# Attention and GLU on one core: GpSimd raises 2 to a power for one score bank in most passes

## The chip, the core and the metric

The kernel runs on one core of a Trainium2 chip. The core has five engines, each with its own in-order stream of instructions: PE (TensorE, matmuls), ACT (ScalarE), DVE (VectorE), POOL (GpSimd) and SP (SyncE, which here only issues DMAs). They meet through semaphores. SBUF is the working memory; PSUM has eight banks of 128 x 512 fp32, into which PE writes. The metric is the device time of one execution in microseconds. Three runs of the kernel before gave a median of 909.52 us (908.95 to 911.22).

## What is computed

The reference, cut to what matters (S = 2048 rows, D = 640, 32 heads of Dh = 20, F = 1728):

```python
xn = layernorm(x)
q, k, v = split(xn @ wqkv)                  # 32 heads of 20
p = softmax(q @ k.T * 20 ** -0.5)           # per head, 2048 x 2048
s = (p @ v) @ wo
h = sigmoid(xn @ w_gate) * (xn @ w_up)
g = silu(h @ w_down)
out = x + s * g
```

The 32 x 2048 x 2048 exponentials of the softmax are the bulk of the elementwise work.

## The kernel before

**Setup.** x is loaded and normalised (statistics on DVE, L226 to L241, the apply on POOL, L245), transposed on PE, and the first projections are made.

**Passes.** The four column chunks of 512 queries (QC) times eight groups of four heads (NG, GH) make 32 passes. A pass has 16 key tiles x 4 heads = 64 score banks (PER_PASS), each one 128 x 512 matmul of K (21 rows) against q (L1035); there are 2,048 banks in all. The scores are scaled so that a probability is 2^(score/128 - 127). Each bank of scores in PSUM is turned into bf16 probabilities in SBUF, and PE multiplies these with V into the accumulator bank `oacc` (L1161), which a pass fills and `normalise` empties (L770).

**Who makes the exponentials.** ACT works in rounds: alternately three and two banks lie in one PSUM tile (`sc`), and one activation with Exp takes them at once (`act_exp`, L1058). Where DVE has room, `issue` scores one bank more in the round, into one of two PSUM banks (`misc0`, `misc1`, named spare or work) that all side jobs share too, and DVE makes 2^x in four operations (`dve_exp`): a maximum that reads PSUM into `dy` (L1069), a square and a cube on the low 16 bits of `dy` into `du` (L1074, L1078), and the sum that writes the bits of the bf16 (L1082). The last three read two operands in SBUF each. `dve_bank` picks the bank.

**Side jobs.** Between rounds PE does fill jobs: the projections of q, k and v, the gate and up matmuls (L643, L656), the down projection (L679), the output projection (L717). Each takes a misc bank, which DVE or ACT frees. The normalised gate result goes to DRAM (`gq_dram`, L699) and is read back (`gqr`, L712, four buffers) for the output, which POOL stores with an accumulating DMA (L726, L757).

**Normalisation of a pass.** `normalise` copies `oacc` to `oev` (L770), sends the denominators to DRAM (`den_dram`, L771), loads them in another shape (`den`, L776), takes reciprocals (L780), sends them to DRAM (`rec_dram`, L781), loads them four times as a broadcast (`rl`, L787), and multiplies (`oT`, L799). All these DMAs are issued by POOL. `oT` has NG + 3 buffers.

**The order.** A planner in the kernel's Python writes out each engine's order by hand. It keeps a clock for PE, ACT and DVE (`Engine`), with a cost for each operation (606 ns for a DVE operation on a bank, MM5 = 216 ns for a matmul of 512 columns, n x 512/1.2 + 52 ns for an activation of n banks, 3,400 ns from a DMA to its use), and emits an instruction when its inputs are there by these clocks. SP loads weights (`wg`, `wu`, L619, L621) and q (`qT`, L608) in the planned order. Where PE has room and has streamed less than ENOUGH (2,300) ns of matmul in the last 3,400 ns, `zero_add` (L1141) adds a matmul with a zero matrix to `oacc` (L1146); it does so only while a pass's accumulation is under way.

Of the kernel before, what the change touches and what calls it, by code (L numbers as in the profile page):

```python
# [15 lines left out]
P = 128  # L16
HEAD = 32
GH = 4
# [15 lines left out]
OCTAVE = 128.0  # L34
ONE = (127.0 + 80.0) * OCTAVE
LEAST = 128.0
EXP_BIAS = -127.0 / LOG2E
# [7 lines left out]
def kernel(  # L45
# [53 lines left out]
    pick = const.tile([P, GH], FP32, name="pick")  # L99
    zero = const.tile([P, P], BF16, name="zero")  # L100

    xnT = persist.tile([P, KD, S], BF16, name="xnT")
# [59 lines left out]
    with tc.tile_pool(name="setup", bufs=1) as sp, \  # L162
# [34 lines left out]
        nc.gpsimd.memset(eps_t, 1e-5)  # L197
        nc.gpsimd.memset(zero, 0.0)
        nc.scalar.activation(out=warm[:, 0:1], in_=eps_t, func=ACT.Sqrt)
        nc.gpsimd.memset(v_all[:, :, 0:VF, 0:1], 1.0)  # L200
# [168 lines left out]
    INTO = {"score": 100.0, "pv": 100.0, "fill": 100.0}  # L369
    WINDOW, ENOUGH = 3400.0, 2300.0  # L370
    PE_OUT, SEM = 260.0, 70.0
# [36 lines left out]

    act, dve = Engine(), Engine()
    pe = [0.0]  # L410
# [6 lines left out]
    def advance(until):  # L417
        while True:
            moved = act.run(until)
            moved = dve.run(until) or moved  # L420
            for x in sorted((x for x in timed if x[0] <= until), key=lambda x: x[0]):
# [244 lines left out]
    def down_job(tt):  # L666
# [25 lines left out]
        def finish():  # L692
            last = c == NQC - 1
            gq = kT_all[:, t4, :].bitcast(FP32)[:, 0:D] if last else d2
            nc.vector.scalar_tensor_tensor(out=gq, in0=made["t"], scalar=1.0, in1=d2, op0=ALU.add, op1=ALU.mult)
            if last:
                gq_last[t4] = gq
            else:
                nc.gpsimd.dma_start(out=gq_dram[tt, :, :], in_=d2)  # L699

# [6 lines left out]
    def out_job(tt):  # L707
        qc, t4 = divmod(tt, QC // P)
        yield "known", lambda: all((qc, g) in ot_cells for g in range(NG)) and (not tt or tt - 1 in out_cells)
        yield "wait", [ot_cells[qc, g] for g in range(NG)] + ([out_cells[tt - 1]] if tt else [])  # L710
        gqr = glu[0].tile([P, D], FP32, tag="gqr", bufs=4, name="gqr")
        nc.sync.dma_start(out=gqr, in_=gq_dram[tt, :, :])  # L712
# [50 lines left out]
    def normalise(qc, g, done):  # L763
        n = qc * NG + g
        cell = ot_cells[qc, g] = Cell()
        t = {}

        def s0():
            t["oev"] = wk.tile([P, QC], FP32, tag="oev", bufs=OBUFS, name="oev")
            nc.vector.tensor_copy(out=t["oev"], in_=oacc)  # L770
            nc.gpsimd.dma_start(out=den_dram[n, :, :], in_=t["oev"][0:P:32, :])  # L771
            at(dve.t + DMA_WAIT, s1)

        def s1():
            t["den"] = wk.tile([P, GH * QC // P], FP32, tag="den", bufs=2, name="den")
            nc.gpsimd.dma_start(out=t["den"], in_=den_dram[n, :, :].rearrange("j (r c) -> (j r) c", c=GH * QC // P))  # L776
            dve.add(250.0, [Cell(pe[0] + DMA_WAIT)], s2, 0)

        def s2():
            nc.vector.reciprocal(out=t["den"], in_=t["den"])  # L780
            nc.gpsimd.dma_start(out=rec_dram[n, :, :].rearrange("j (r c) -> (j r) c", c=GH * QC // P), in_=t["den"])  # L781
            at(dve.t + DMA_WAIT, s3)

        def s3():
            t["rl"] = wk.tile([P, QC], FP32, tag="rl", bufs=OBUFS, name="rl")
            for j in range(GH):
                nc.gpsimd.dma_start(out=t["rl"][32 * j:32 * j + 32, :],  # L787
                                    in_=rec_dram[n, j:j + 1, :].to_broadcast([32, QC]))
            at(pe[0] + DMA_WAIT + LANDED, s4)

        def s4():
            if g >= 3 and qc and not all(out_cells.get(tt, Cell()).t for tt in range((qc - 1) * 4, qc * 4)):
                at(pe[0] + 300.0, s4)
                return
            dve.add(606.0, [], s5, 2)

        def s5():
            oTs[qc, g] = wk.tile([P, QC], BF16, tag="oT", bufs=NG + 3, name="oT")
            nc.vector.tensor_tensor(out=oTs[qc, g], in0=t["oev"], in1=t["rl"], op=ALU.mult)  # L799
            cell.t = dve.t + 114.0  # L800
# [174 lines left out]
    KEEP_SPARE, KEEP_LATE, SPARE_END, next_round = 800.0, 400.0, 20 * PER_PASS, [0.0]  # L975
    BUFS, D_BACKLOG = {3: 4, 2: 4, 1: 3}, 2500.0
    NEEDED, NEEDED_LAST = 6, 12
# [61 lines left out]
    class Probs:  # L1039

        def __init__(self, banks, tag):
            self.n, self.left, self.tag = len(banks), len(banks), tag
            self.made, self.used = None, Cell()
            self.before = buffers[self.n].pop(0)
            buffers[self.n].append(self.used)
            for i, b in enumerate(banks):
                insort(ready_p[b % GH], (b, self, i), key=lambda x: x[0])

        def tile(self):
            self.ap = pp.tile([P, self.n, 512], BF16, tag=self.tag, bufs=BUFS[self.n], name=self.tag)  # L1050
            return self.ap
# [11 lines left out]
    def dve_exp(ps, b, begun):  # L1063
# [26 lines left out]
        return first  # L1090

    def issue():
        ci = chunk[0]
# [5 lines left out]
        if (ci > 1 and dve.backlog + max(0.0, dve.t - pe[0]) < D_BACKLOG  # L1099
                and all(c.t is not None for c in d_made[-2:-1])):  # L1100
            extra = dve_bank(taken)
            if extra is not None:
# [6 lines left out]
        if split:  # L1109
            score(split[1], extra)  # L1110
            issued(extra)
            give_bank(split[0], dve_exp(split[1], extra, begun))
            n += 1
# [5 lines left out]
    def pv_batch():  # L1119
# [68 lines left out]
    while pv_pass[0] < len(steps):  # L1188
# [46 lines left out]
        if zero_add(room):  # L1235
            idle = False
            continue
        soon = [q[k][1].made.t for q in ready_p for k in range(min(2, len(q)))]
        times = [until, pe[0] + 150.0] + [t + SEM for t in soon if t is not None]
# [32 lines left out]
    nc.vector.tensor_copy(out=rb, in_=rq.unsqueeze(3).to_broadcast([P, QC // P, GH, 32]))  # L1272
    oT = wk.tile([P, QC], BF16, tag="oT", bufs=NG + 3, name="oT")
    oTs[qc, g] = oT
# [9 lines left out]
    for bank, (t4, h) in zip(banks, units):  # L1284
# [5 lines left out]
        if h == 1:  # L1290
            if t4 % 2 == 0:
                pair = glu[0].tile([P, D], FP32, tag="gqr", bufs=4, name="ot").bitcast(BF16)
            ot = pair[:, t4 % 2 * D:(t4 % 2 + 1) * D]
# [30 lines left out]
```

## Time and profile before

One profiled execution took 909.74 us, of which 907.8 us are the span from the first instruction to the last. Its mean granted TensorE clock was 0.986.

| engine | busy us | share of the span | instructions |
|---|---|---|---|
| ACT | 871.8 | 96% | 837 |
| DVE | 839.6 | 92% | 1,480 |
| PE | 795.1 | 88% | 6,020 |
| POOL | 161.7 | 18% | 305 |

| group | count | mean ns |
|---|---|---|
| ACT Exp on three banks (L1058) | 358 | 1,575 |
| ACT Exp on two banks (L1058) | 359 | 1,148 |
| DVE maximum, square, cube, sum of a bank (L1069 to L1082) | 256 each | 681 to 683 |
| PE zero matmul (L1146) | 92 records of 129 | 388 |
| POOL apply in the setup (L245), 128 x 640 | 16 | 873 |
| POOL issue of `rl` (L787) | 124 | 522 |

A group's line gives its line in the kernel, engine, operation, out<-in with shapes and count; then the busy time and the mean of one; then the time that the engine sat idle just before the group, and what ended most of it. Activations overlap at their ends, so the two means exceed the busy time per activation. In the slices and windows a digit or number is the engine's busy time in that stretch; PEclk is the clock granted to PE, 1.00 being full. The chain is followed back from the last instruction to what released each step.

### The profile page before, as it was taken

The page shows a single profiled execution, that of the slowest core. Times are in us where ns is not written, and L with a number is a line of the kernel's source. Part 1 is how long each engine was busy: PE and PEld are TensorE (multiplying, and loading weights), DVE is VectorE, ACT ScalarE, POOL GpSimd, SP SyncE. Part 2 cuts the span into 40 slices and gives each one's busy share as a digit, 9 for nine tenths or more (in the row PEclk, how much of TensorE's full clock was granted, in tenths as well). Part 3 has the DMA queues.
Part 4 walks back from the last instruction along what each step waited for, and adds up shares of the span by engine and source line. Part 5 has one row for each costly group of instructions (what it writes and reads, how often), then busy time and mean ns, then how long its engine had stood idle before and what let it go on. Part 6 is the DMA issues. An engine that isn't in the chain of part 4 may idle for free.

```text
span 907.8 us, 16427 instructions
## 1 busy us (share of the span) xinstructions
PE 795.1 (88%) x6020; PEld 278.3 (31%) x6091; DVE 839.6 (92%) x1480; ACT 871.8 (96%) x837; POOL 161.7 (18%) x305
## 2 busy tenths in 40 slices
PE   5898989999888998989899988888989888989884
PEld 3334333222222332222233332222332232233232
DVE  7799999978999999998999998987999998999994
ACT  6999999988999999999999999999999999999992
POOL 7401111101111122111102221101112221111130
PEclk9999999977999999999999999999999999999998
DMA  8112231254232134313212243213112334200021
GB/s 312 46 41 80 74 98 35 69 166 136 70 78 56 36 106 62 72 43 90 52 35 77 77 72 78 63 34 73 34 52 76 90 62 88 57 19 14 14 59 41
DMA packets 105894, 64.36 MB, mean 71 GB/s; under 512 B 79982, under 2 KB 100002, under 8 KB 105594
## 3 DMA queue, kind: packets, MB, share of 16 engines
q1 hardware_dynamic: 95606, 47.21, 19.3%
q0 software_dynamic: 10208, 16.11, 7.7%
q8 instruction: 47, 0.77, 0.3%
q14 instruction: 33, 0.27, 0.1%
HBM read 50.45 MB, written 16.13 MB: 73 GB/s over the span
## 4 chain that ended last, share of the span: by engine, by line
ACT 55%; issue 17%; PE 14%; DVE 10%; POOL 1%; DMA 1%; SPq 0%; ACTq 0%; DVEq 0%; POOLq 0%
ACT p L1058 51%; PE sc L1035 5%; PE oacc L1161 3%; ACT tnh L650 3%; DVE dy L1069 2%; PE work L643 2%; DVE du L1074 2%; PE work L679 1%; DVE du L1078 1%; PE work L656 1%; DVE p L1082 1%; ACT td L690 1%; PE work L123 1%; DVE stats L226 1%; DMA den<-den_dram 1%
## 5 line engine op out<-in xcount | busy, mean ns | idle before, releaser
L1058 ACT ACTIVATE p<-sc 128x1536 bf16<-128x1536 f32 x717 | 828.9, 1361 | 10.3 <-PE sc L1035 4.5
L1035 PE MATMUL sc<-qT,kT_all 21*128 21x512 bf16 x1792 | 281.9, 386 | 74.8 <-ACT p L1058 68.8
L1069 DVE TENSOR_SCALAR dy<-spare 128x512 f32<-128x512 f32 x256 | 174.8, 683 | 26.0 <-PE spare L1035 24.1
L1035 PEld LDWEIGHTS <-kT_all 21*128 21x128 bf16 x2048 | 87.5, 91 | 308.5 <-issue 297.1
L1078 DVE SCALAR_TENSOR_TENSOR du<-du,dy 128x512 f32<-128x512 f32 x256 | 173.9, 682 | 1.8
L1082 DVE SCALAR_TENSOR_TENSOR p<-du,dy 128x512 uint16<-128x512 f32 x256 | 173.8, 681 | 1.8
L1074 DVE SCALAR_TENSOR_TENSOR du<-dy 128x512 f32<-128x512 uint16 x256 | 173.6, 682 | 0.7
L1161 PE MATMUL oacc<-p,v_all 128*21 128x512 bf16 x2048 | 159.1, 386 | 0.8 <-issue 0.5
L1035 PE MATMUL spare<-qT,kT_all 21*128 21x512 bf16 x256 | 99.1, 387 | 0.3 <-DVE gqr L723 0.3
L771 POOL DMA_DIRECT2D den_dram<-oev x31 | 18.0, 580 | 392.2 <-DVE oev L770 392.2
L679 PE MATMUL work<-wd,hT 128*128 128x320 bf16 x448 | 84.9, 302 | 1.2 <-DVE dy L1069 0.8
L643 PE MATMUL work<-xnT,wg 128*128 128x512 bf16 (+1 forms) x260 | 78.2, 387 | 1.5 <-DVE hT L660 0.4
L656 PE MATMUL work<-xnT,wu 128*128 128x512 bf16 (+1 forms) x267 | 76.5, 384 | 2.3 <-DVE dy L1069 0.9
L787 POOL DMA_DIRECT2D rl<-rec_dram x124 | 62.2, 522 | 54.7 <-DMA rec_dram<-den 45.7
L679 PEld LDWEIGHTS <-hT 128*128 128x128 bf16 x448 | 35.4, 97 | 48.1 <-issue 38.4
L1161 PEld LDWEIGHTS <-v_all 128*21 128x21 bf16 x2048 | 29.7, 90 | 64.3 <-issue 62.6
L660 DVE SCALAR_TENSOR_TENSOR hT<-tnh,work 128x512 bf16<-128x512 bf16 (+1 forms) x56 | 38.0, 679 | 6.0 <-PE work L656 3.5
L650 ACT ACTIVATE tnh<-work 128x512 bf16<-128x512 f32 (+1 forms) x56 | 40.9, 731 | 0.0
L781 POOL DMA_DIRECT2D rec_dram<-den x31 | 16.9, 546 | 133.0 <-DVE den L780 128.4
L717 PE MATMUL work<-wo_pad,oT 128*128 128x320 bf16 x192 | 35.5, 301 | 1.3 <-DVE dy L1069 0.7
L123 PE MATMUL work<-xnT,wqd 128*120 128x512 bf16 (+1 forms) x115 | 35.8, 406 | 0.8 <-DVE kd L499 0.4
L656 PEld LDWEIGHTS <-wu 128*128 128x128 bf16 (+1 forms) x280 | 23.1, 98 | 39.9 <-issue 25.9
(109 smaller groups left out, 538.8 us busy)
## 6 DMA issues: line engine op xcount, KB each, us to landing
wg<-in_B_w_gate_dram SPq DMA_DIRECT2D x52, 160.0 KB
wu<-in_B_w_up_dram SPq DMA_DIRECT2D x52, 160.0 KB
rl<-rec_dram POOLq DMA_DIRECT2D x124, 64.0 KB, 2.3
qT<-q_dram SPq DMA_DIRECT2D x31, 128.0 KB
gq_dram<-d POOLq DMA_DIRECT2D x12, 320.0 KB, 2.5
gqr<-gq_dram SPq DMA_DIRECT2D x12, 320.0 KB
kT_all<-k_dram SPq DMA_DIRECT2D x28, 128.0 KB
wd<-in_B_w_down_dram SPq DMA_DIRECT2D x1, 2080.0 KB
```

The source lines that it names most:

```text
L643: nc.tensor.matmul(psg[0:fsz, :], lhsT=wg[:, kd, 0:fsz], rhs=xnT[:, kd, cols], start=(kd == 0), stop=(kd == KD - 1))
L650: nc.scalar.activation(out=made["t"][0:fsz, :], in_=psg[0:fsz, :], func=ACT.Tanh, scale=0.5)
L656: nc.tensor.matmul(psu[0:fsz, :], lhsT=wu[:, kd, 0:fsz], rhs=xnT[:, kd, cols], start=(kd == 0), stop=(kd == KD - 1))
L679: nc.tensor.matmul(psd[:, 0:HALF], lhsT=hT[0:fsz, kf, t4 * P:(t4 + 1) * P], rhs=glu[1][0:fsz, kf, e0_:e1_], start=(kf == 0), stop=(kf == N ...
L787: nc.gpsimd.dma_start(out=t["rl"][32 * j:32 * j + 32, :], in_=rec_dram[n, j:j + 1, :].to_broadcast([32, QC]))
L1035: nc.tensor.matmul(ps, lhsT=kT_all[32 * j:32 * j + 1 + Dh, g, kt * P:(kt + 1) * P], rhs=qTs[qc, g][32 * j:32 * j + 1 + Dh, :], start=True, ...
L1058: nc.scalar.activation(out=buf.tile(), in_=ps, func=ACT.Exp, bias=EXP_BIAS, scale=exp_scale)
L1069: nc.vector.tensor_scalar(out=t["y"], in0=ps, scalar1=LEAST, scalar2=None, op0=ALU.max)
L1074: nc.vector.scalar_tensor_tensor(out=t["u"], in0=t["f"], scalar=CUBE_2, in1=t["f"], op0=ALU.add, op1=ALU.mult)
L1078: nc.vector.scalar_tensor_tensor(out=t["u"], in0=t["u"], scalar=CUBE_1, in1=t["f"], op0=ALU.add, op1=ALU.mult)
L1082: nc.vector.scalar_tensor_tensor(out=buf.tile()[:, 0, :].bitcast(U16), in0=t["u"], scalar=CUBE_SCALE, in1=t["y"], op0=ALU.mult, op1=ALU.add)
L1161: nc.tensor.matmul(oacc[32 * j:32 * j + 1 + Dh, :], lhsT=v_all[:, b % PER_PASS // GH, GH * g + j, 0:1 + Dh], rhs=buf.ap[:, i, :], start=(n ...
```

## The change

POOL takes one score bank in a pass, where the planner lets it. `issue` asks `pool_bank` first: it offers a bank only after the 40th round, with POOL free, and only if 400 ns for each bank left in the pass cover POW (20,000 ns, the planner's cost of the power) plus 3,000. Then DVE makes one operation (`px` = score/128 - 127, fp32, in SBUF) and POOL one: `pw` = 2 to the power `px`, with a column of twos as the base. `pw` has one buffer and is a kind of its own (0); `pv_batch` passes over such a bank until its planned end.

The DMAs of `normalise` (L771, L776, L781, L787) and the store of `gq_dram` (L699) are issued by SP instead of POOL. The accumulating stores stay on POOL. `gqr` has three buffers instead of four, and `oT` NG + 2 instead of NG + 3; `normalise` holds back its last step from the third group on (g >= 2, it was 3) until the chunk before is put out.

ENOUGH is 2,500 instead of 2,300. `zero_add` also runs when no accumulation is under way: into `oacc` if it is free, else into a free misc bank.

```diff
+POW = 20000.0
+    two = const.tile([P, 1], FP32, name="two")
+        nc.gpsimd.memset(two, 2.0)
-    WINDOW, ENOUGH = 3400.0, 2300.0
+    WINDOW, ENOUGH = 3400.0, 2500.0
-    act, dve = Engine(), Engine()
+    act, dve, pool = Engine(), Engine(), Engine()
-                nc.gpsimd.dma_start(out=gq_dram[tt, :, :], in_=d2)
+                nc.sync.dma_start(out=gq_dram[tt, :, :], in_=d2)
-        gqr = glu[0].tile([P, D], FP32, tag="gqr", bufs=4, name="gqr")
+        gqr = glu[0].tile([P, D], FP32, tag="gqr", bufs=3, name="gqr")
-            nc.gpsimd.dma_start(out=den_dram[n, :, :], in_=t["oev"][0:P:32, :])
+            nc.sync.dma_start(out=den_dram[n, :, :], in_=t["oev"][0:P:32, :])
...
-            if g >= 3 and qc and not all(out_cells.get(tt, Cell()).t for tt in range((qc - 1) * 4, qc * 4)):
+            if g >= 2 and qc and not all(out_cells.get(tt, Cell()).t for tt in range((qc - 1) * 4, qc * 4)):
-            oTs[qc, g] = wk.tile([P, QC], BF16, tag="oT", bufs=NG + 3, name="oT")
+            oTs[qc, g] = wk.tile([P, QC], BF16, tag="oT", bufs=NG + 2, name="oT")
-    BUFS, D_BACKLOG = {3: 4, 2: 4, 1: 3}, 2500.0
+    BUFS, D_BACKLOG = {3: 4, 2: 4, 1: 3, 0: 1}, 2500.0
...
+    def pool_exp(ps, b, begun):
+        buf = Probs([b], "pw")
+        t = {}
+
+        def copy():
+            t["x"] = pp.tile([P, 512], FP32, tag="px", bufs=1, name="px")
+            nc.vector.tensor_scalar(out=t["x"], in0=ps, scalar1=1.0 / OCTAVE, scalar2=-127.0, op0=ALU.mult, op1=ALU.add)
+
+        def power():
+            nc.gpsimd.tensor_tensor(out=buf.tile()[:, 0, :], in0=two.to_broadcast([P, 512]), in1=t["x"], op=ALU.pow)
+
+        first = dve.add(606.0, [Cell(begun + MM5 + PE_OUT - 100.0), *pow_made[-1:]], copy, 0, 114.0)
+        buf.made = pool.add(POW, [first, buf.before], power, 0, 200.0)
+        pow_made.append(buf.made)
+        return first
+
+    pow_made = []
+
+    def pool_bank(banks):
+        if pool.queue or pool.t > pe[0] + 1000.0 or any(c.t is None or c.t > pe[0] + 1000.0 for c in pow_made[-1:]):
+            return None
+        b = min((x for x in coming(GH) if x not in banks), default=None)
+        if b is None or b >= NB - PER_PASS:
+            return None
+        if 400.0 * (PER_PASS - b % PER_PASS) < POW + 3000.0:
+            return None
+        return b
...
-            extra = dve_bank(taken)
+            extra = pool_bank(taken) if ci > 40 else None
+            maker = dve_exp if extra is None else pool_exp
+            if extra is None:
+                extra = dve_bank(taken)
...
-            give_bank(split[0], dve_exp(split[1], extra, begun))
+            give_bank(split[0], maker(split[1], extra, begun))
...
+                if buf.kind == 0 and not (buf.made.t is not None and buf.made.t + SEM <= pe[0]):
+                    continue
...
-        if streamed() >= ENOUGH or not 0 < sum(pv_count[0]) < GH * KT:
+        if streamed() >= ENOUGH or (0.0 if mode[0] == "fill" else INTO["fill"]) + MM5 > room:
             return False
-        if (0.0 if mode[0] == "fill" else INTO["fill"]) + MM5 > room:
-            return False
-        nc.tensor.matmul(oacc, lhsT=zero, rhs=xnT[:, 0, 0:QC], start=False, stop=False, skip_group_check=True)
+        begun = 0 < sum(pv_count[0])
+        if begun and sum(pv_count[0]) < GH * KT or not begun and oacc_free[0].t is not None and oacc_free[0].t <= pe[0]:
+            nc.tensor.matmul(oacc, lhsT=zero, rhs=xnT[:, 0, 0:QC], start=not begun, stop=not begun, skip_group_check=True)
+        else:
+            free = [i for i in range(2) if banks[i].t is not None and banks[i].t <= pe[0]]
+            if not free:
+                return False
+            ps = psum.tile([P, QC], FP32, tag=f"misc{free[0]}", bufs=1, name="unused")
+            nc.tensor.matmul(ps, lhsT=zero, rhs=xnT[:, 0, 0:QC], start=True, stop=True)
         pe_do("fill", MM5)
         return True
```

In the changed kernel's line numbers the four DVE operations are L1074, L1079, L1083 and L1087, the copy to `px` is L1103, and the power L1106.

More of the change, by code (lines that the diff above doesn't have):

```diff
@@ L420, in advance @@
             moved = dve.run(until) or moved
+            moved = pool.run(until) or moved
             for x in sorted((x for x in timed if x[0] <= until), key=lambda x: x[0]):
@@ L775, in s1 @@
             t["den"] = wk.tile([P, GH * QC // P], FP32, tag="den", bufs=2, name="den")
-            nc.gpsimd.dma_start(out=t["den"], in_=den_dram[n, :, :].rearrange("j (r c) -> (j r) c", c=GH * QC // P))
+            nc.sync.dma_start(out=t["den"], in_=den_dram[n, :, :].rearrange("j (r c) -> (j r) c", c=GH * QC // P))
             dve.add(250.0, [Cell(pe[0] + DMA_WAIT)], s2, 0)
@@ L780, in s2 @@
             nc.vector.reciprocal(out=t["den"], in_=t["den"])
-            nc.gpsimd.dma_start(out=rec_dram[n, :, :].rearrange("j (r c) -> (j r) c", c=GH * QC // P), in_=t["den"])
+            nc.sync.dma_start(out=rec_dram[n, :, :].rearrange("j (r c) -> (j r) c", c=GH * QC // P), in_=t["den"])
             at(dve.t + DMA_WAIT, s3)
@@ L786, in s3 @@
             for j in range(GH):
-                nc.gpsimd.dma_start(out=t["rl"][32 * j:32 * j + 32, :],
+                nc.sync.dma_start(out=t["rl"][32 * j:32 * j + 32, :],
                                     in_=rec_dram[n, j:j + 1, :].to_broadcast([32, QC]))
@@ L1042, in __init__ @@
             self.n, self.left, self.tag = len(banks), len(banks), tag
+            self.kind = self.n if tag != "pw" else 0
             self.made, self.used = None, Cell()
-            self.before = buffers[self.n].pop(0)
-            buffers[self.n].append(self.used)
+            self.before = buffers[self.kind].pop(0)
+            buffers[self.kind].append(self.used)
             for i, b in enumerate(banks):
@@ L1049, in tile @@
         def tile(self):
-            self.ap = pp.tile([P, self.n, 512], BF16, tag=self.tag, bufs=BUFS[self.n], name=self.tag)
+            self.ap = pp.tile([P, self.n, 512], BF16, tag=self.tag, bufs=BUFS[self.kind], name=self.tag)
             return self.ap
@@ L1237 @@
             continue
-        soon = [q[k][1].made.t for q in ready_p for k in range(min(2, len(q)))]
+        soon = [q[k][1].made.t for q in ready_p for k in range(min(3, len(q)))]
         times = [until, pe[0] + 150.0] + [t + SEM for t in soon if t is not None]
@@ L1272 @@
     nc.vector.tensor_copy(out=rb, in_=rq.unsqueeze(3).to_broadcast([P, QC // P, GH, 32]))
-    oT = wk.tile([P, QC], BF16, tag="oT", bufs=NG + 3, name="oT")
+    oT = wk.tile([P, QC], BF16, tag="oT", bufs=NG + 2, name="oT")
     oTs[qc, g] = oT
@@ L1291 @@
             if t4 % 2 == 0:
-                pair = glu[0].tile([P, D], FP32, tag="gqr", bufs=4, name="ot").bitcast(BF16)
+                pair = glu[0].tile([P, D], FP32, tag="gqr", bufs=3, name="ot").bitcast(BF16)
             ot = pair[:, t4 % 2 * D:(t4 % 2 + 1) * D]
```

## The prediction

> **What bounds the kernel now.** I read the page's busy shares, its slices and its chain first, then the groups, then windows by time.
>
> ```profile
> PE 795.1 (88%) x6020; PEld 278.3 (31%) x6091; DVE 839.6 (92%) x1480; ACT 871.8 (96%) x837; POOL 161.7 (18%) x305
> ACT  6999999988999999999999999999999999999992
> PEclk9999999977999999999999999999999999999998
> ACT 55%; issue 17%; PE 14%; DVE 10%; POOL 1%; DMA 1%; SPq 0%; ACTq 0%; DVEq 0%; POOLq 0%
> ...
> L1058 ACT ACTIVATE p<-sc 128x1536 bf16<-128x1536 f32 x717 | 828.9, 1361 | 10.3 <-PE sc L1035 4.5
> L1069 DVE TENSOR_SCALAR dy<-spare 128x512 f32<-128x512 f32 x256 | 174.8, 683 | 26.0 <-PE spare L1035 24.1
> ```
>
> ACT's exponentials are the path: 828.9 us for the 1,792 banks that ACT takes, 0.4626 us a bank, 1.156 us a round of 2.5 banks. From 226.9 to 885.1 us ACT is idle for about 1.8 us in all (22.70 less the busy time, summed over those windows). DVE is close behind: a bank on DVE is four operations of 682 ns, 2.73 us. One stretch is different:
>
> ```profile
> 191.00:194.00 3.00, 2.07 (x18) 0.70 (x18) 3.00 (x7) 3.00 (x4) 0.00 (x0) 0.87 0.08 28
> 194.00:197.00 3.00, 2.72 (x8) 0.84 (x8) 2.68 (x6) 1.64 (x3) 0.58 (x1) 0.50 0.82 185
> ...
> 209.00:212.00 3.00, 2.67 (x19) 0.61 (x16) 2.85 (x5) 2.47 (x2) 0.10 (x1) 0.50 0.37 93
> 212.00:215.00 3.00, 3.00 (x20) 0.54 (x19) 1.51 (x4) 2.10 (x2) 1.88 (x4) 0.72 0.33 87
> 215.00:218.00 3.00, 2.69 (x24) 0.72 (x20) 2.97 (x6) 3.00 (x4) 0.00 (x0) 1.00 0.29 66
> ```
>
> The columns are window, length, busy time of PE, PEld, DVE, ACT and POOL, then granted clock, DMA share and GB/s. For 20 us the clock is 0.50, and ACT idles 6.2 us of the 24 from 191 to 215. That is what one loss of clock costs here.
>
> **What GpSimd's port does to DVE.** In the main part of before, POOL issues DMAs only. Only the setup has POOL instructions that read SBUF beside DVE instructions with two SBUF inputs (nb is made from mv and rstd). In the timeline (start, duration):
>
> ```profile
> 8.67 2.58 POOL L245 TENSOR_SCALAR x_sb<-x_sb,rstd,nb 128x640 bf16<-128x640 bf16 x3 [2.08 <-DVE rstd L240]
> ...
> 8.96 0.59 DVE L241 SCALAR_TENSOR_TENSOR nb<-mv,rstd 128x1 f32<-128x1 f32 x1
> ...
> 11.01 0.24 DVE L241 SCALAR_TENSOR_TENSOR nb<-mv,rstd 128x1 f32<-128x1 f32 x1
> ...
> 20.74 1.73 POOL L245 TENSOR_SCALAR x_sb<-x_sb,rstd,nb 128x640 bf16<-128x640 bf16 x2 [0.53 <-DVE nb L241]
> ...
> 20.98 0.64 DVE L241 SCALAR_TENSOR_TENSOR nb<-mv,rstd 128x1 f32<-128x1 f32 x1
> ```
>
> Alone nb takes 0.16 us. One POOL operation takes 0.86 to 0.87, so the first of the three at 8.67 ends at 9.54 and nb at 9.55; the third ends at 11.25, and so does the nb that started at 11.01; the first at 20.74 ends at 21.61 and nb at 21.62. It is the same where nb starts at 13.62 and 18.17: five times out of five, a DVE instruction that starts inside a POOL instruction ends 0.00 to 0.02 us behind it. The longest hold was 0.48 us. The Trainium skill (SBUF — State Buffer, "Who interferes with whom") says that a DVE instruction with two SBUF inputs and a GpSimd instruction that reads SBUF exclude each other for the whole instruction. These five rows agree; none shows it for a long instruction.
>
> **The change, part by part.** The order of the changed program's instructions gives the counts.
>
> 1. ACT: 1,782 banks instead of 1,792 (4 activations fewer). 10 x 0.4626 = **-4.6 us**, on the path.
>
> 2. DVE: 244 banks by the four operations instead of 256, -12 x 2.73 = -32.7 us; 22 copies to px of about 0.68 us (the dy row, same form), +15.0 us. Net -17.7 us, nothing by itself while ACT ends last. So 22 powers on POOL relieve ACT of only 10 banks; the other 12 come off DVE.
>
> 3. The power, 22 times on POOL. The trace of before has none. From below: POOL's 640-element tensor_scalar at 0.87 us, 0.70 us for 512 elements. From above: the planner's own figure, 20 us, times the 682/606 by which DVE's rows exceed the planner's, 22.5 us. I take 20: the planner's figures for compute lie at or below their rows (606 against 682, a pair of activations 2,237 against 2,312, tanh 480 against 740), so nothing suggests that it is far too high; with the margin of its DMA wait (3,400 against landings of 2.3 us at the median) it would be 13.5. The skill's price for a plain two-input add (GPSIMD Engine Reference, "Elementwise — side-by-side cycle accounting") is 4,497 ns at 2,048 elements; an estimate from it is 1.1 us for 512, and at that length the sum would be about -4.6 us, for a hold of 22 x 1.1 us is paid out of DVE's 17.7.
>
> 4. What the power holds up. Three of a DVE bank's four operations (L1074, L1078, L1082) read two SBUF operands, as do oT (L799) and d (L695). In the new order the first of these stands directly behind the px copy in 11 of 22 places, four back at most. I take it that what the five rows show also holds for a long instruction: DVE stops within a few operations and stays stopped until the power ends. Behind it in order stand PSUM banks to be freed and probabilities that PE waits for. Following PE's order from the power's own score matmul to the first instruction that needs a stopped DVE operation gives 2 to 8 rounds, 4.6 on average; 4.6 x 1.156 = 5.3 us of work for ACT. Matmul, copy and hand-over (0.39 + 0.68 + 0.2) use 1.3 of it before the power starts, and about one round scored earlier (1.2) is still in ACT's hands: ACT stops about 5 us into the power. Restarting takes one DVE operation, one matmul (0.39) and their hand-overs, about 1.5 us. Loss: 20 - 5 + 1.5 = 16.5 us a power, **+363 us** for 22. With 13.5 us a power it is +220, with 22.5 +418.
>
> 5. The clock after such stops. Bounds: nothing (in the first 22.7 us PE idles 6.6 us before its first matmul, and the mean clock is 1.00), and 6.2 us (the event at 193 us), for each of 22. I take 2 us, nearer to the setup since the held work is ready when DVE comes back: **+44 us**. The skill (TensorE: Matmul & The Clock Gate, Part 1) lets the clock return after one busy window of 3.4 us; by that, a sixth of the event's price, 22 x 1.1 = 24 us. The event disagrees: PE was busy 2.6 to 3.0 of each 3 us, and the clock stayed at 0.50 for 20.
>
> 6. Zeros: 218 matmuls instead of 129, in gaps that the planner sees. 89 x 0.39 us of PE beside ACT's work, cost nothing unless they delay a score (a fifth of a us each at worst). They may prevent the event at 193 us (three fall in the rounds around the first gate matmul, where before had one behind it): between 0 and -6.2. I count 0, because stops of 16 us undo any such help.
>
> 7. DMAs: 229 (31 x 7 + 12) move from POOL's queue to SP's. There den waits for den_dram, rec for DVE, rl for rec_dram, each about 2 us (landing 1.7 to 2.3), and weight and qT loads stand behind them. They cost nothing as long as the planner's 3.4 us between steps covers it, and POOL no longer carries 115 us of issuing. 16 accumulating stores stay on POOL, some right behind a power; gqr has 3 buffers instead of 4, so the gqr load three later waits on SP for such a store. oT loses one buffer. I count 0 beside the stops; alone it is a rival below.
>
> Sum against the profiled execution's 909.74 us (span 907.8, 1.9 around it; the runs' median, 909.52, is the same within 0.03%): 909.7 - 4.6 + 363 + 44 = **1312 us**. This forecast's own range, from the ends of points 3 and 5, is 1125 to 1459.
>
> **Rivals.**
>
> *The hold is not for a whole long instruction.* All five holds lie in POOL instructions that stream, 1.36 ns an element; a power of 20 us takes 39 ns an element and leaves the port free most of the time. If port and DVE share by element, or the power takes its input early, DVE loses nearly nothing and ACT gains. Then 909.7 - 4.6 = 905.1, and 898.9 if the zeros also save the event at 193 us: faster. This decides the sign; also a power below about 5 us, which the 5.3 us of scored work covers. For it: 22 holds of 20 us would take half of DVE's time, and no row shows a hold over 0.48 us. Against it: five of five rows, each held to the end.
>
> *SP's and POOL's queues.* No hold, but stores wait up to 20 us behind a power, and gqr loads with weights, qT and normalisation behind them on SP. Seven places in POOL's order have a store right behind a power; if three of them hold PE for 5 to 10 us each: 905 + 15 to 30, 920 to 935.
>
> *The power is longer than planned.* Each is due 3 us before its pass ends; at 25 us, without any hold, PE waits 2 us or more for pw at the end of 22 passes: about 950.
>
> *The change does little.* The 4.6 us are eaten by lost slots: 907 to 912.
>
> **How the numbers follow.** Hold for the whole power 0.45; faster rival 0.36 (half near 905, half near 899); queues or a late power 0.14; little 0.05. A difference under 0.3% (2.7 us) can't be told from none here: faster 0.36, same 0.05, slower 0.59. The range takes the forecast up to 1400 (leaving out 0.06 above) and goes down to 899 (leaving out some 0.1): both signs are in it, because one unknown separates them.
>
> **What would show it.** Right: L1079, L1083 and L1087 of the new kernel with a maximum of 10 us or more, ending within 0.02 us of a pw instruction; ACT idle near 16 us in each of 22 passes; clock below 1 behind each. Wrong: those lines at 682 ns throughout while pw runs, and ACT idle as before. Wrong in size alone: pw at another length than 20 us. The queue rival would show as SP waiting for an accumulating store and PE waiting for weights or qT.

## The result, and the profile after

The changed kernel takes 2,290.79 us (median of 4 runs, 2,282.47 to 2,295.49); the kernel before took 910.02 beside it (908.95 to 911.22). The ratio is 2.516 [2.508, 2.525]. It is slower, as forecast, and 979 us above the 1,312 us of the forecast, far outside the range.

The same lines of the page, now of the changed kernel (busy times, two slices, the granted clock, the chain by engine, and five groups):

```profile
PE 914.8 (40%) x6180; PEld 294.1 (13%) x6180; DVE 836.2 (36%) x1454; ACT 881.3 (38%) x833; POOL 1847.6 (81%) x99
...
ACT  8908080440431422508044043172625044043177
POOL 4494949989889899885898989929497999988920
PEclk9958585775765756758577576586767567576689
...
POOL 76%; PE 8%; issue 6%; ACT 5%; DVE 4%; DMA 0%; SPq 0%; DVEq 0%; POOLq 0%; ACTq 0%
...
L1106 POOL TENSOR_TENSOR pw<-two,px 128x512 bf16<-128x512 f32 x22 | 1806.6, 82119 | 332.2 <-DVE px L1103 332.2
L1063 ACT ACTIVATE p<-sc 128x1536 bf16<-128x1536 f32 x713 | 829.5, 1284 | 1322.0 <-PE spare L1039 735.7
L1205 PE MATMUL oacc<-pw,v_all 128*21 128x512 bf16 x22 | 12.9, 585 | 1301.2 <-POOL pw L1106 1301.2
L1074 DVE TENSOR_SCALAR dy<-spare 128x512 f32<-128x512 f32 x244 | 166.3, 683 | 816.0 <-PE spare L1039 814.5
...
L1087 DVE SCALAR_TENSOR_TENSOR p<-du,dy 128x512 uint16<-128x512 f32 x244 | 169.8, 699 | 1.7
```

ACT and DVE are as busy as before, about 880 and 836 us; the span has grown around them. The chain now stands 76% on POOL. A power takes **82,119 ns**, four times the planner's 20,000. The third group is the whole story: the 22 PV matmuls that read `pw` kept PE waiting 1,301.2 us, 59.1 each, and while PE stands, ACT gets no scores (1,322 us idle). The last line bears on the prediction's test, which was a longest operation of 10 us or more: L1087 still has a mean of 699 ns (L1083 has 687). By instruction (count, shortest/median/longest ns):

```profile
L1087 DVE SCALAR_TENSOR_TENSOR p<-du,dy x244: 621/683/1412, 37.7 to 2268.2; 128x512 uint16<-128x512 f32 x122
```

The longest of L1083 is 1.35 us and of L1079 0.70, so DVE was *not* stopped for the length of a power.

The timeline around the first power (start us, length us, engine, line, operation) shows both halves:

```profile
86.18 82.27 POOL L1106 TENSOR_TENSOR pw<-two,px 128x512 bf16<-128x512 f32 x1 [51.73 <-DVE px L1103]
...
85.94 0.68 DVE L1083 SCALAR_TENSOR_TENSOR du<-du,dy 128x512 f32<-128x512 f32 x1
86.66 1.41 DVE L1087 SCALAR_TENSOR_TENSOR p<-du,dy 128x512 uint16<-128x512 f32 x1
87.99 0.68 DVE L1074 TENSOR_SCALAR dy<-spare 128x512 f32<-128x512 f32 x1
...
90.96 0.68 DVE L1083 SCALAR_TENSOR_TENSOR du<-du,dy 128x512 f32<-128x512 f32 x1
91.56 0.88 DVE L158 CAST v_all<-work 128x480 bf16<-128x480 f32 x2
92.35 0.68 DVE L1087 SCALAR_TENSOR_TENSOR p<-du,dy 128x512 uint16<-128x512 f32 x1
...
168.50 0.59 PE L1205 MATMUL oacc<-pw,v_all 128*21 128x512 bf16 x1 [57.17 <-POOL pw L1106]
```

One DVE operation with two SBUF operands is held: L1087, started 0.48 us after the power, takes 1.41 instead of 0.68. The next ones, 5 and 6 us in, run at 0.68 while the power goes on for another 76. In 9 of the 22 powers one such operation is held, and it ends 1.58 to 1.97 us after the power's start. Then PE meets the matmul that reads `pw` in its order and stands 57.17 us, with ready matmuls of other banks behind it. The same stretch in windows (window, length, busy time of PE, PEld, DVE, ACT and POOL, granted clock, DMA share, GB/s):

```profile
124.00:144.00 20.00, 0.00 (x0) 0.00 (x0) 0.00 (x0) 0.00 (x0) 20.00 (x1) 0.50 0.00 0
168.00:176.00 8.00, 7.50 (x35) 1.72 (x35) 3.66 (x7) 3.52 (x4) 0.45 (x1) 0.50 0.01 2
176.00:186.00 10.00, 10.00 (x44) 2.49 (x43) 4.78 (x9) 6.40 (x6) 0.00 (x0) 0.50 0.24 70
186.00:196.00 10.00, 9.82 (x61) 2.89 (x59) 8.40 (x17) 8.60 (x8) 0.00 (x0) 0.78 0.29 77
196.00:206.00 10.00, 9.14 (x72) 3.44 (x71) 10.00 (x18) 10.00 (x10) 1.04 (x1) 1.00 0.30 83
```

From 124 to 144 us only POOL works. The clock is 0.50 then, and stays there for about 20 us after PE resumes at 168.5.

**The account.** With the power's 22 operations replaced by a short one (e1_mult below) the kernel takes 929.2 us. 2,290.8 - 929.2 = 1,361.6 us. PE's wait for `pw` (in the profiled execution) is 1,301.2 of it; 60.4 are left, 2.7 us a power. The slow clock and the restart lie in these; no run separates them. The slack between a power's start and PE's need is 82.1 - 59.1 = 23.0 us on average.

### The profile page after: what moved, and what is told of

The parts are those of the page before. It is cut to its first block, busy times and chain, and to the rows that moved or that the text cites. A ratio compares the mean times of both kernels' runs of the same rounds, so it can differ in the third digit from the quotient of the medians.

```text
span 2291.5 us, 16638 instructions
## 1 busy us (share of the span) xinstructions
PE 914.8 (40%) x6180; PEld 294.1 (13%) x6180; DVE 836.2 (36%) x1454; ACT 881.3 (38%) x833; POOL 1847.6 (81%) x99
## 3 DMA queue, kind: packets, MB, share of 16 engines
q1 hardware_dynamic: 112462, 60.04, 9.7%
q0 software_dynamic: 2304, 3.28, 1.2%
## 4 chain that ended last, share of the span: by engine, by line
POOL 76%; PE 8%; issue 6%; ACT 5%; DVE 4%; DMA 0%; SPq 0%; DVEq 0%; POOLq 0%; ACTq 0%
POOL pw L1106 76%; ACT p L1063 5%; PE sc L1039 2%; PE oacc L1205 2%; PE work L660 1%; PE work L125 1%; PE work L647 1%; PE work L683 1%; DVE dy L1074 1%; DVE px L1103 1%; DVE du L1079 0%; DVE p L1087 0%; DVE du L1083 0%; PE oacc L1184 0%; DVE stats L229 0%
## 5 line engine op out<-in xcount | busy, mean ns | idle before, releaser
L1106 POOL TENSOR_TENSOR pw<-two,px 128x512 bf16<-128x512 f32 x22 | 1806.6, 82119 | 332.2 <-DVE px L1103 332.2
L1205 PE MATMUL oacc<-pw,v_all 128*21 128x512 bf16 x22 | 12.9, 585 | 1301.2 <-POOL pw L1106 1301.2
L1074 DVE TENSOR_SCALAR dy<-spare 128x512 f32<-128x512 f32 x244 | 166.3, 683 | 816.0 <-PE spare L1039 814.5
L1039 PE MATMUL sc<-qT,kT_all 21*128 21x512 bf16 x1782 | 297.1, 412 | 33.3 <-ACT p L1063 29.0
L1205 PE MATMUL oacc<-p,v_all 128*21 128x512 bf16 x2026 | 182.8, 419 | 1.2 <-DVE p L1087 1.0
L1087 DVE SCALAR_TENSOR_TENSOR p<-du,dy 128x512 uint16<-128x512 f32 x244 | 169.8, 699 | 1.7
L1083 DVE SCALAR_TENSOR_TENSOR du<-du,dy 128x512 f32<-128x512 f32 x244 | 166.9, 687 | 2.0
L1079 DVE SCALAR_TENSOR_TENSOR du<-dy 128x512 f32<-128x512 uint16 x244 | 165.6, 683 | 1.1
L1039 PE MATMUL spare<-qT,kT_all 21*128 21x512 bf16 x266 | 109.4, 411 | 3.9 <-DVE hT L664 2.6
L1103 DVE TENSOR_SCALAR px<-spare 128x512 f32<-128x512 f32 x22 | 15.2, 690 | 254.5 <-PE spare L1039 254.5
L647 PE MATMUL work<-xnT,wg 128*128 128x512 bf16 (+1 forms) x280 | 90.6, 427 | 5.0 <-DVE dy L1074 2.2
L660 PE MATMUL work<-xnT,wu 128*128 128x512 bf16 (+1 forms) x280 | 89.5, 436 | 2.9 <-DVE dy L1074 2.4
L687 DVE COPY d<-work 128x320 f32<-128x320 f32 x32 | 15.4, 482 | 182.6 <-PE work L683 182.5
L1184 PE MATMUL oacc<-xnT,zero 128*128 128x512 bf16 x218 | 78.4, 409 | 1.2 <-DVE oev L774 1.2
```

Of the source, the lines that this page charges most:

```text
L647: nc.tensor.matmul(psg[0:fsz, :], lhsT=wg[:, kd, 0:fsz], rhs=xnT[:, kd, cols], start=(kd == 0), stop=(kd == KD - 1))
L660: nc.tensor.matmul(psu[0:fsz, :], lhsT=wu[:, kd, 0:fsz], rhs=xnT[:, kd, cols], start=(kd == 0), stop=(kd == KD - 1))
L1039: nc.tensor.matmul(ps, lhsT=kT_all[32 * j:32 * j + 1 + Dh, g, kt * P:(kt + 1) * P], rhs=qTs[qc, g][32 * j:32 * j + 1 + Dh, :], start=True, ...
L1074: nc.vector.tensor_scalar(out=t["y"], in0=ps, scalar1=LEAST, scalar2=None, op0=ALU.max)
L1079: nc.vector.scalar_tensor_tensor(out=t["u"], in0=t["f"], scalar=CUBE_2, in1=t["f"], op0=ALU.add, op1=ALU.mult)
L1083: nc.vector.scalar_tensor_tensor(out=t["u"], in0=t["u"], scalar=CUBE_1, in1=t["f"], op0=ALU.add, op1=ALU.mult)
```

## The experiments

Two theories stood when the result was known. *The hold*: POOL's power shuts DVE out of its second SBUF port for its length (the forecast's mechanism, with the longer power). *The late power*: DVE runs, and PE waits in order for a result that comes 59 us late. And one question beside them: what do the other parts of the change cost without the power?

### The change without a long power: e1_mult, e2_no_bank, e3_quarter

```diff
# e1_mult: the same 22 instructions, another operation (these 22 banks then hold no probabilities)
-            nc.gpsimd.tensor_tensor(out=buf.tile()[:, 0, :], in0=two.to_broadcast([P, 512]), in1=t["x"], op=ALU.pow)
+            nc.gpsimd.tensor_tensor(out=buf.tile()[:, 0, :], in0=two.to_broadcast([P, 512]), in1=t["x"], op=ALU.mult)
# e2_no_bank: POOL gets no bank
-            extra = pool_bank(taken) if ci > 40 else None
+            extra = None
# e3_quarter: the power on 128 of the 512 columns, the multiplication on 384
+            nc.gpsimd.tensor_tensor(out=pw[:, 0, 0:128], in0=two.to_broadcast([P, 128]), in1=t["x"][:, 0:128], op=ALU.pow)
+            nc.gpsimd.tensor_tensor(out=pw[:, 0, 128:512], in0=two.to_broadcast([P, 384]), in1=t["x"][:, 128:512], op=ALU.mult)
```

> Everything of the change stays, in the same order, but POOL multiplies px by two instead of raising 2 to it (the 22 banks then hold no probabilities). Theory A, that PE's wait for the 82 us of pw makes the whole loss and the rest of the change is sound: the multiplication takes 1 to 2 us, PE never waits for it, and the time is 898 to 907 us (909.7 less 4.6 us of ACT, less up to 6.2 us if the clock holds at the first gate matmul). Theory R, that the moved DMAs and the smaller buffers cost as well: above 912. The forecast's hold of DVE by POOL (H) expects here what A expects, since the POOL instruction is short.

> Everything of the change but the power: no bank goes to POOL; the DMAs on SP, the smaller buffers and the added zeros stay. A: 902 to 911 us (909.7, less up to 6.2 if the zeros keep the clock at the first gate matmul). R: above 912. Beside e1_mult it gives what the 22 banks are worth if their power cost nothing: A expects about 4.6 us more here than there.

> POOL raises 2 to the power for 128 of the 512 columns and multiplies the other 384 (those hold no probabilities), so that the POOL work of a bank takes about 82.1/4 = 20.5 us and 1 more, which is near the 20 us that the planner allows. A: as e1_mult within 1%, 898 to 915 us, with DVE's two-operand operations at 682 ns but for one hold of some 0.3 us per power. H, the forecast's point 4: DVE stands for most of each power, 22 x 16.5 us, and the time is above 1200 us.

Measured: e1_mult 929.23 us, ratio 1.021 [1.017, 1.025]; e2_no_bank 932.0, 1.024 [1.019, 1.028]; e3_quarter 941.0, 1.033 [1.029, 1.038]. e3 is the forecast's own case, a power of the planned 20 us. Its `pw` tile (count, shortest/median/longest ns) and who waited for it:

```profile
L1107 POOL TENSOR_TENSOR pw<-two,px x22: 20717/20912/21226, 85.3 to 817.8; 128x128 bf16<-128x128 f32 x22
...
  PE oacc L1207: 9.8, 11
```

A power of 20.9 us, 22 times, was to cost 363 us through the hold. It costs 941.0 - 929.2 = 11.8, and 9.8 of that are PE's wait for `pw` in 11 places. So the hold for the whole power is out, at the length for which it was forecast. What hold there is, e1's short multiplication (1.03 to 1.55 us) causes as well. In e1 the operation held by the first of them, at 85.41 us, is the one that the first power of the changed kernel holds (at 86.66 there), and it takes the same time:

```profile
85.89 1.41 DVE L1087 SCALAR_TENSOR_TENSOR p<-du,dy 128x512 uint16<-128x512 f32 x1
```

In e1 too there are 9 such places of 22, the same ones, and the held operation ends 1.58 to 1.97 us after the start: for DVE, 82 us of power are no more than 1.2 of multiplication.

e1 and e2 show a second thing, by which theory A of the expectations (898 to 915) missed in all three runs and R came true: without any long power the rest of the change loses some 20 us. The 22 banks on POOL, even as cheap as 1.23 us, give back some 3 (the two intervals overlap).

### The operation by itself: m1_size

A small stand-alone program: POOL operations one at a time, then four of them beside a row of DVE operations with one and with two SBUF operands in turn.

> A program by itself (it computes nothing of the reference; the output is a copy of x): POOL powers of 512, 128 and 32 columns, of 16 partitions, and with an fp32 result, then multiplications, each alone; then powers of 128 and 64 columns and multiplications of 1024 and 2048 columns beside a row of DVE operations with one and with two operands. A: the power's time goes with the columns, 82, 20.5 and 5.1 us; beside a power DVE's two-operand operations wait at its start only, for well under 1 us, and beside a multiplication that reads all the time they wait to its end (1 to 5 us). H: they wait to the end of the power too, 20 and 10 us.

Its timeline (221.42 us in all):

```profile
3.15 81.92 POOL L82 TENSOR_TENSOR y<-two,x 128x512 bf16<-128x512 f32 x1 [2.32 <-DVE x L66]
85.36 20.72 POOL L82 TENSOR_TENSOR y<-two,x 128x128 bf16<-128x128 f32 x1 [0.29 <-DVE x L78]
106.37 5.42 POOL L82 TENSOR_TENSOR y<-two,x 128x32 bf16<-128x32 f32 x1 [0.29 <-DVE x L78]
112.07 20.72 POOL L82 TENSOR_TENSOR y<-two,x 16x128 bf16<-16x128 f32 x1 [0.29 <-DVE x L78]
...
154.08 1.26 POOL L89 TENSOR_TENSOR y<-x 128x512 bf16<-128x512 f32 x1 [0.29 <-DVE x L78]
...
158.81 20.72 POOL L106 TENSOR_TENSOR y<-two,x 128x128 bf16<-128x128 f32 x1 [0.84 <-DVE x L97]
...
191.35 2.34 POOL L108 TENSOR_TENSOR y<-x 128x1024 bf16<-128x1024 f32 x1 [1.04 <-DVE x L97]
...
159.47 0.69 DVE L101 SCALAR_TENSOR_TENSOR d<-d 128x512 f32<-128x512 f32 x1
160.19 0.69 DVE L100 TENSOR_SCALAR d<-ps 128x512 f32<-128x512 f32 x1
160.92 0.69 DVE L101 SCALAR_TENSOR_TENSOR d<-d 128x512 f32<-128x512 f32 x1
...
191.96 2.28 DVE L101 SCALAR_TENSOR_TENSOR d<-d 128x512 f32<-128x512 f32 x1
```

The power needs 81.92 us for 512 columns, 20.72 for 128, 5.42 for 32: (81.92 - 20.72) / 384 = 0.159 us a column, and the same on 16 partitions as on 128. A multiplication of the same shape takes 1.26. The length is the operation's own; nothing in the kernel stretches it. And the two kinds of POOL operation treat DVE differently: beside the power of 128 columns every two-operand operation (L101) takes its 0.69 us; beside the multiplication of 2.34 us the one that starts at 191.96 takes 2.28 and ends 0.55 us after POOL, which ends at 193.69 (beside a 3.60-us multiplication: 3.54, 0.54 behind POOL).

### Dose and place of the wait: e5_half, e8_every4, e7_unread

```diff
# e5_half: as e3_quarter, with 256 columns of power and 256 of multiplication
# e8_every4: a bank for POOL in every fourth pass only (7 powers of full length)
-        if b is None or b >= NB - PER_PASS:
+        if b is None or b >= NB - PER_PASS or b // PER_PASS % 4:
# e7_unread: as e8_every4, and PV of those banks reads another tile than pw
-                                 rhs=buf.ap[:, i, :], start=(n == 0), stop=(n == KT - 1),
+                                 rhs=buf.ap[:, i, :] if buf.kind else xnT[:, 0, 0:QC], start=(n == 0), stop=(n == KT - 1),
```

> As e3_quarter, with the power for 256 columns (41.2 us) and the multiplication for the other 256. A: PE waits for pw for whatever exceeds the 23.0 us that lie on average between the power's start and PE's need (82.1 less 1301.2/22 = 59.1), so 22 x (41.7 - 23.0) = 411 us, and some 60 for the clock and restarts as in the changed kernel (2290.8 - 929.2 - 1301.2): about 1400 us. If the loss went in proportion to POOL's time instead: 929 + 1362/2 = 1610.

> The changed kernel with a bank for POOL in every fourth pass only: 7 powers of 512 columns. A: 7 x (59.1 + 2.8) = 433 us above e2_no_bank's 932, about 1365 us.

> As e8_every4, but the matmuls of those 7 banks read a tile of xnT in the place of pw (so 7 banks count wrongly); POOL still makes the 7 powers of 82 us, and nobody waits for them. A: the whole loss of e8_every4 goes, 925 to 940 us, unless an accumulating store that stands behind a power on POOL holds a gqr load on SP (71.5 us once in the changed kernel): then up to 1000. H, that the power holds DVE's port: 7 x 75 us remain, about 1450.

One run each, so without an interval: 1,411.04, 1,376.54 and 987.67 us. The matmuls that read `pw`, in e5 and then in e8 (idle time before them at the end of the line):

```profile
L1207 PE MATMUL oacc<-pw,v_all 128*21 128x512 bf16 x22 | 12.9, 584 | 414.6 <-POOL pw L1108 414.6
```

```profile
L1205 PE MATMUL oacc<-pw,v_all 128*21 128x512 bf16 x7 | 4.1, 585 | 413.8 <-POOL pw L1106 413.8
```

In e5 POOL needs 41.3 + 0.6 = 41.9 us a bank and PE waits 18.8; in e8 82.0 and 59.1. The slack is 23.1, 22.9, and 23.0 in the changed kernel: on average the wait is (length - 23) a power, at 42 us as at 82 and for 7 powers as for 22. The slack varies from place to place, since e3 waits in 11 of 22 places at 20.9 + 0.9 = 21.8 us. What is left beside this wait is 67 us above e1 in e5, 3.1 a power, and 31 above e2 in e8, 4.4 a power, so that the 2.7 of the changed kernel is no constant. e7 keeps seven powers of 82 us beside DVE, which the hold would charge with 7 x 78.6 = 550 us, and takes away only PE's reading of them: 389 us of e8's 1,376.5 go. That settles it for PE's wait. e7 is still 58 us above e1, more than the 925 to 940 expected without stores in the way. Its waits (total us, times, longest):

```profile
DVE gqr L727 <- DMA gqr<-gq_dram: 56.0, 2, 30.7
...
SPq L716 <- DMA out_dram<-gqr: 54.1, 2, 29.0
```

In two places SP waits, 54.1 us in all, to load `gqr`, since its buffer is still to be stored by an accumulating DMA that POOL issues, and POOL is in a power. That is the queue rival's mechanism, twice in the run, seen where PE's wait doesn't cover it.

### The rest of the change: f1_dma, f2_zeros, f3_bufs, f4_back

f1 to f3 put one part of the change each into the kernel before; f4 is e1_mult with the DMAs put back on POOL.

```diff
# f1_dma (five such lines: L699, L771, L776, L781, L787 of before); f4_back is the reverse
-                nc.gpsimd.dma_start(out=gq_dram[tt, :, :], in_=d2)
+                nc.sync.dma_start(out=gq_dram[tt, :, :], in_=d2)
# f2_zeros: the new zero_add, and
-    WINDOW, ENOUGH = 3400.0, 2300.0
+    WINDOW, ENOUGH = 3400.0, 2500.0
# f3_bufs: gqr 4 to 3 buffers, oT NG + 3 to NG + 2, g >= 3 to g >= 2
```

> The kernel before with only the DMAs of the normalisation and the store of gq_dram moved from POOL's queue to SP's. Theory Q, that the transfers then stand behind the 4 MB of wd and out that SP issues at 193 us (in e2_no_bank DVE's reciprocal waited 10.2 us there for den) and behind weight loads: 920 to 932 us, most of the 20 us by which e2_no_bank is slower. Theory S, that the smaller buffers and the later oT make it: within 3 us of 910.

> The kernel before with only the zeros changed (ENOUGH 2500, also into free banks). The forecast's point 6 gave 0 to -6.2 us: 903 to 910, the lower end if the clock holds at the first gate matmul. If the added matmuls delay scores: 911 to 916.

> The kernel before with only the smaller buffers (gqr 3, oT NG + 2) and the last step of the normalisation held back from the third group on. S: 918 to 930 us. Q: within 3 us of 910.

> e1_mult (all of the change, POOL multiplying px by two instead of raising 2 to it, so that 22 banks hold no probabilities) with the DMAs of the normalisation and of gq_dram back on POOL's queue. Q: 900 to 912 us, about 20 less than e1_mult. S: within 5 us of e1_mult's 929.

| kernel | us | ratio |
|---|---|---|
| f1_dma | 922.56 | 1.014 [1.008, 1.020] |
| f2_zeros | 905.57 | 0.995 [0.992, 0.997] |
| f3_bufs | 912.90 | 1.005 [1.002, 1.009] |
| f4_back | 907.88 | 0.997 [0.994, 1.000] |

The DMAs on SP are the largest loss; the zeros alone gain and **beat both kernels**. f4 bounds what POOL's banks could give in this order: with an operation of 1.23 us in place of the power, the DMAs left on POOL and the zeros in, it is 0.3% or nothing, and f2, without those banks, is 2.3 us faster than f4.

f2 gains in two places. The first, in windows of f2, then of before:

```profile
186.00:230.00 44.00, 37.75 (x259) 11.57 (x263) 38.57 (x69) 39.84 (x39) 5.05 (x10) 0.96 0.55 164
```

```profile
186.00:230.00 44.00, 40.12 (x236) 9.97 (x237) 36.54 (x65) 37.80 (x36) 4.44 (x9) 0.77 0.52 158
```

The clock is 0.96 instead of 0.77 and ACT works 2.0 us more in this stretch: the loss of clock at 193 us is mostly gone, and that is some two of the 4.5 us. But this is one execution of each. The profiled execution of f3, which has no added zeros, shows a clock of 0.88 and ACT busy for 39.91 us here, so that the zeros keep the clock in this place is not shown. The second place is at full clock (1.00 in both): ACT works 82.09 of the first 92 us in f2, 80.17 in before. There ACT waits in before for scores that stand in PE's order behind 33 matmuls of a fill job:

```profile
85.72 5.67 ACT L1058 ACTIVATE p<-sc 128x1024 bf16<-128x1024 f32 x5 [1.71 <-PE spare L1035]
```

f1 and f3 have the same wait of 1.71 us, f2 and f4 don't. So this gain comes from the order, which the planner makes anew around the added matmuls, and not from the clock.

Where f1 loses: ACT idles 13.9 us of 184 to 230 (6.2 before) and 6.1 of the next 92 us (0.6 before). At this spot SP issues the first gate and up weights and 4 MB of `wd` and `out`. The timeline of f1:

```profile
196.15 1.26 SPq L887 DMA_DIRECT2D wd<-in_B_w_down_dram  x1
197.46 0.70 SPq L889 DMA_DIRECT2D out_dram<-in_A_x_dram  x1
198.21 0.58 SPq L619 DMA_DIRECT2D wg<-in_B_w_gate_dram  x1
198.83 2.08 SPq L621 DMA_DIRECT2D wu<-in_B_w_up_dram  x1
201.01 5.87 SPq L550 DMA_DIRECT2D q_dram<-qd  x1
206.92 0.45 SPq L776 DMA_DIRECT2D den<-den_dram  x1
...
212.13 0.25 DVE L780 RECIPROCAL den<-den 128x16 f32<-128x16 f32 x1 [7.92 <-DMA den<-den_dram]
```

and of before, where POOL issues the same load:

```profile
197.96 0.56 POOL L776 DMA_DIRECT2D den<-den_dram  x1 [3.04 <-DMA den_dram<-oev]
...
200.50 6.29 SPq L550 DMA_DIRECT2D q_dram<-qd  x1
...
205.82 0.24 DVE L780 RECIPROCAL den<-den 128x16 f32<-128x16 f32 x1
```

With transfers piled up, one issue holds SP for about 6 us, in both kernels. Before, the `den` load left POOL at 197.96 and had no need to wait for SP; now it stands behind that issue on SP, leaves at 206.92, and DVE's reciprocal, 6.3 us later than before, stops DVE for 7.92 us in its order, with banks behind it.

### Taking the 4 MB out of SP's way: f5_wd_pool, f6_wd_act

```diff
# f1_dma, and (f5: gpsimd, f6: scalar) for the two wd loads and the copy into out
-        nc.sync.dma_start(out=wd[:, 0:nf, :], in_=B_w_down[0:nf * P, :].rearrange("(f p) d -> p f d", p=P))
+        nc.gpsimd.dma_start(out=wd[:, 0:nf, :], in_=B_w_down[0:nf * P, :].rearrange("(f p) d -> p f d", p=P))
```

> f1_dma with the loads of wd and the copy of x to out (4 MB, issued at the start of the gate stage) put on POOL's queue, so that the normalisation's small transfers on SP do not stand behind them. Q: the 8 to 10 us wait of DVE for den there goes, 908 to 915 us. If it is SP's order as such: it stays at 920 to 924.

> f1_dma with wd and the copy of x to out issued by ACT in their planned place (on POOL, in f5_wd_pool, nothing held them and they started at 34 us, onto the first projections). Q: DVE's wait for den at the gate stage (7.9 us in f1_dma) goes and nothing else moves: 908 to 916 us. If the transfers stand behind the 4 MB whoever issues them: 920 to 924, the wait as in f1_dma.

f5 takes 926.13 us, 1.017 [1.015, 1.020]; f6 922.38, 1.014 [1.010, 1.018]; neither mends f1. In f5 the wait for `den` is gone and ACT's idle time from 186 to 330 us is 6.8, as before the change (f1: 20.0); but POOL, with nothing ahead of them, starts the 4 MB at 34 us, where DVE waits 8.1 us for `k_dram` and ACT's idle time in the first 92 us is 22.8 instead of 11.8. In f6 ACT issues them at the planned place, DVE waits for `den` for 0.9 us at most, and the timeline shows another victim:

```profile
203.23 1.03 PE L643 MATMUL work<-xnT,wg 128*128 128x512 bf16 x2 [8.17 <-DMA wg<-in_B_w_gate_dram]
```

The wait has moved from `den` to the gate weights. Which share is SP's order and which the transfers that all share stays open. The move also takes the transfers from one DMA queue to another (q0 has 10,208 packets in before and 2,304 in f1, q1 95,606 and 112,462), and no run tries that alone. The Trainium skill (DMA: Bandwidth & Descriptors, "Issuing engines are not separate DMA queues") says that DMAs of all issuing engines run on the same 16 engines and that another issuer saves only the issuing time. f6 agrees, 922.38 beside 922.56; f1 against before shows how far the issuing time can go on a loaded queue, 5.87 us for one issue.

### The normalisation behind a power: f7_quarter_pool

e3_quarter with the DMAs of `normalise` and `gq_dram` back on POOL, by the same five lines as f4: what does their move to SP buy while POOL computes for 21 us?

> e3_quarter (power for 128 columns, 21.8 us on POOL, 384 columns multiplied) with the DMAs of the normalisation and of gq_dram back on POOL's queue, behind the powers. If a normalisation is late by one power in most passes, oacc is not free for the next pass: above 1000 us. If they mostly fall between the powers: 915 to 960.

1,323.2 us in one run, against 941.0 with SP. Its largest wait:

```profile
DVE den L784 <- DMA den<-den_dram: 366.2, 22, 19.7
```

DVE waits 16.6 us for `den` in each of 22 places, since POOL issues the store of the denominators, and then that load, behind a power. So the move to SP costs 21 us where POOL is free (e1 against f4, 929.23 and 907.88) and saves 382 where POOL is taken: it belongs to the power.

## Why the prediction was wrong, point by point

**Point 3, the power's length, is the term that failed.** The prediction took the planner's 20 us and let 22.5 stand as the upper end, because the planner's other figures "lie at or below their rows (...), so nothing suggests that it is far too high"; that other operations agree was no evidence for one without a row. The power takes 82.1 us: 62 more, 22 times.

**Point 4, the hold, failed as a mechanism.** The five rows it rested on were read rightly, and m1 shows the same in multiplications of 2.34 and 3.60 us. The step that failed is "I take it that what the five rows show also holds for a long instruction". The power holds DVE at its start only, about as long as a multiplication of 512 columns does (e1: the same 9 places, the same 1.41 us beside the first), and then leaves it alone; that fits an instruction which reads its input first and then computes, as the first rival had it ("or the power takes its input early"), though no run shows the reading itself. The Trainium skill (SBUF — State Buffer, "Who interferes with whom") speaks of an exclusion for the whole instruction: the multiplications agree, the power doesn't.

**The rival "the power is longer than planned" is what happened**, at another size. It said that a power is due 3 us before its pass ends, a slack of 20 + 3 = 23 us; the runs give 23.0. With 82.1 in place of its 25 us, and with the 44 us of point 5, it would have given 905.1 + 22 x 59.1 + 44 = 2,249; measured 2,290.8. The hold with 82.1 us would have given 22 x (82.1 - 5 + 1.5) = 1,729 and 2,678. So the direction came out right by luck, by a mechanism that isn't there: with the planned 20 us and no hold, e3 loses 11.8 us, not 363.

**Point 5, the clock.** 2 us a power were taken; 2.7 is what is left for clock and restart together, which the runs don't separate. The clock stays at 0.50 for some 20 us of mostly busy PE, as at 193 us in before, so the return after one busy window of 3.4 us that the prediction cited from the Trainium skill (TensorE: Matmul & The Clock Gate, Part 1) does not show here either (PE busy for 7.50 of 8 and 10.00 of 10 us at 0.50).

**Points 1 and 2.** ACT makes 713 activations and DVE 244 banks with 22 copies, as counted. Of the 4.6 us forecast for ACT's 10 banks e2 to e1 shows 2.8, with overlapping intervals. The aside in point 3, that a hold of 22 x 1.1 us is paid out of DVE's 17.7, doesn't add up: it is 24.2.

**Point 6, the zeros,** was counted 0 with bounds 0 and -6.2; alone they give -0.5% [-0.8, -0.3], inside. The reason given, the event at 193 us, can be at most a part: some two of the 4.5 us lie there, and as much lies before 92 us at full clock.

**Point 7, the DMAs and buffers,** was counted 0 and costs some 20 us with the zeros. Its rival had the size, 920 to 935, and placed it behind powers; all of f1's loss lies where SP's own weight loads stand (ACT idle of 184 to 322 us: 19.9, before 6.8). The parts add up to 1.4 + 0.5 - 0.5 = 1.4% against e2's 2.4%: 1%, about 9 us, is in how they act together. It lies later: of 322 to 820 us ACT idles 14.7 in e2, beside 1.1 in before, 1.8 in f1 and 5.7 in f3. There DVE waits 5.3 us for `gqr` and 6.3 for `rl` in e2, and 0 and 0.6 in f1. That points to the smaller buffers together with the loads on SP; no run has these two alone, so the cause stays open.

## What to carry to other kernels

Before an operation without a row in the trace enters a plan, measure it alone at two sizes; a planner's own figure is no upper bound. For work handed to a slow engine, set its length against the slack until the in-order consumer reaches the result: beyond the slack every microsecond is paid, as often as it is done. An issue moved to another engine stands behind all that this engine issues, so look at that queue's fullest moment, not at its mean.

## What the runs showed of the hardware that was not expected

- A power on POOL costs 0.159 us a column on 16 partitions as on 128, and with an fp32 result as with a bf16 one (20.73 and 20.72 us); a multiplication of 128 x 512 costs 1.26.
- POOL shuts DVE's two-operand operations out to the end of a multiplication (2.28 us for an operation of 0.69), but beside a power of 82 us a held operation ends 1.58 to 1.97 us after its start, as beside a multiplication of the same 512 columns.
- One DMA issue held SP for 5.87 us while the transfers before it were piled up; the usual one of its kind took 0.69.
